# Attention with an ELU layer on one core: the first batch in slots of two heads by nine tokens, the ELU of thirteen chunks without GpSimd, chunk 0 in halves, MB in two products, another order of words

## The chip, the cores and the metric

The kernel runs on one core of a Trainium2 chip. TensorE (PE) multiplies matrices into eight PSUM banks, VectorE (DVE), ScalarE (ACT) and GpSimd (POOL) work on elements, SyncE (SP) issues DMAs, and GpSimd and ScalarE can issue them too. Each engine works through its own queue in the order in which the program was written, and waits at semaphores for the others. The metric is the device time of one execution in microseconds. All tensors that go in and out are float32.

## The reference

```python
def _attn_ref(q, k, v):                       # each 8 x 8 x 576 x 64: batch, head, token, dim
    q_s = np.exp(q - np.max(q, axis=-1, keepdims=True))
    q_s = q_s / (np.sum(q_s, axis=-1, keepdims=True) + 1e-09)
    k_s = np.exp(k - np.max(k, axis=2, keepdims=True))
    k_s = k_s / (np.sum(k_s, axis=2, keepdims=True) + 1e-09)
    kv = np.einsum('bhsd,bhse->bhde', k_s, v)
    return np.einsum('bhsd,bhde->bhse', q_s, kv)

def _moe_ref(x, w_in, w_out):                 # x 4608 x 512, w_in 512 x 2048, w_out 2048 x 512
    h = x @ w_in
    g = np.where(h > 0.0, h, np.exp(np.minimum(h, 0.0)) - 1.0)
    return g @ w_out
```

Attention here has a softmax of q over the 64 dims of a token, and a softmax of k over the 576 tokens; the 64 x 64 product of k and v is formed first, for each head. The eight heads of a token are then joined to a row of 512, and two dense layers with an ELU between them follow.

## The kernel before

One program, written out by a generator class. The work goes batch by batch (8), and for each batch its dense layers go in 16 chunks of 128 hidden columns. Of a batch's 576 tokens, 512 go through the dense layers as the main block; the remaining 64 of all batches are gathered in XTR and go through them together as a ninth block at the end.

A chunk has three stages. `hidden` (L757): four products of a 128x128 piece of w_in (W1S) with the 512 columns of XT, summed in one of three PSUM banks; then ScalarE takes the exponential into ES, and GpSimd subtracts one (L767). `elu` (L784): VectorE forms min(max(h, 0), ES) into GT, rounded to fp32r. `project` (L793): four products of GT with w_out (W2S) into four banks that stay open over all 16 chunks. The projection of a chunk stands three chunks (LAG = 3) behind its hidden products in TensorE's queue. At the end of a batch `store` copies four banks out and issues four DMAs on SyncE.

The attention of batch j+1 is woven into the chunks of batch j. The tables FIRST, SECOND and LATER give for each chunk three strings of words: done after the hidden products, after the projection, and after `elu`. A word is one step, and may name part and engine: `qmax`, `qsub`, `qexp`, `qsum`, `qmul` are the softmax of q; `kmax`/`peak`, `kturn`, `kacross`, `ksub`, `kexp` that of k; `vconv` turns v to bf16 and sets ones beside it (so that the sum of k comes out of the product); `kv` is the product of k and v, `kfac` divides it by the sum and writes MB, a 128x128 matrix for two heads with zeros off the diagonal (L552 to L566, by a mask, one operation for two heads); `turn`/`pturn` and `wide`/`pwide` turn q to QT by DMA or TensorE; `att`/`flat` multiply MB and QT, and `xc`/`xflat` copy the result to XT. `load` issues a DMA, `w1` and `w2` issue weight loads on GpSimd, `hold` makes SyncE wait for the hidden products just written.

Nothing can be multiplied before batch 0 has its attention, so the string START (L38) orders that head alone. There all q, k, v come in two halves of four heads, with four tokens beside each other in a partition (runs of 1 KB), and the last 64 tokens in separate loads with runs of 256 bytes. The maximum of k over the tokens is taken with VectorE (L299 to L312), turned by TensorE (L328), reduced (L337), put on a diagonal (`diag`) and subtracted in PSUM: `kraw` copies k there by a product with the identity (L471), `kmin` adds the negated maximum (L479, L488). Four products on ones (`warm`) stand between. Batch 1's q waits on SyncE for QS of batch 0 (`await:sp:QS0`). The first four chunks (EARLY = 4) begin their first two hidden products in the head (`h`), as soon as XT 0 and XT 1 are copied; XT 2 and XT 3 follow.

Weights come through GpSimd's own DMA queue in the order of the words `w1:c0:c1` and `w2:c0:c1`; a chunk of either is 262 KB.

## Time and profile before

| what | value |
|---|---|
| median of three runs | 311.13 us (310.7 to 311.62) |
| profiled execution | 311.19 us, span 309.4 us, granted clock 0.999 |
| TensorE busy | 295.6 us (96%), 1605 instructions |
| VectorE busy | 242.7 us (78%) |
| ScalarE busy | 177.2 us (57%) |
| GpSimd busy | 173.7 us (56%) |
| DMA | 51.63 MB, mean 167 GB/s over the span |

The span runs from the first to the last instruction; the time of the execution has 1.8 us more around it. A busy share is a mean over stages with different limits: a head in which all engines work for batch 0, then blocks of 16 chunks with the next batch's attention woven in, then two blocks with less beside the dense layers, and the last stores. DMA is full in the first quarter and mostly idle in the last.

In rows of the timeline the columns are start, duration, engine, line, operation, output and input, the number of merged instructions, and in brackets the idle time before with what ended it. In rows of groups they are busy time, mean nanoseconds of one, idle time. PEld is the loading of weights into TensorE.

### The profile page before, as it was taken

To read this page: it belongs to the slowest core of one execution; us is meant where nothing else is said; L and a number is where in the kernel's file an instruction comes from. 1 tells how busy PE (TensorE), PEld (TensorE's weight loads), DVE (VectorE), ACT (ScalarE), POOL (GpSimd) and SP (SyncE) were. 2 spreads that over 40 slices of the span, in tenths; PEclk is the share of its full clock that TensorE was granted. 3 is DMA by queue.
4 is the path that set the end of the run, shared out by engine and by line. 5 is a ranking of instruction groups with operands and counts; after the bars stand their busy time and mean duration, and the time that the engine had idled before them with its cause. 6 is when DMAs were issued, how large, how long until landed. Compare 5 with 4: busy or idle time off the path is not lost.

```text
span 309.4 us, 4558 instructions
## 1 busy us (share of the span) xinstructions
PE 295.6 (96%) x1605; PEld 236.6 (76%) x1605; DVE 242.7 (78%) x422; ACT 177.2 (57%) x295; POOL 173.7 (56%) x229
## 2 busy tenths in 40 slices
PE   3688998999999999999999999999999999999995
PEld 1356875778878888888888888788888888888884
DVE  6999998999969998999799979997995354335442
ACT  1475785567456755695469547855695543334432
POOL 2987985575546754675467636763676333333440
PEclk9999999999999999999999999999999999999999
DMA  7999999999408986656665666651422030003003
GB/s 236 319 352 328 373 337 308 250 286 237 153 11 229 260 201 162 210 149 173 176 212 148 157 192 196 160 147 52 170 36 42 2 136 0 0 2 137 0 1 136
DMA packets 65608, 51.63 MB, mean 167 GB/s; under 512 B 29361, under 2 KB 58289, under 8 KB 65585
## 3 DMA queue, kind: packets, MB, share of 16 engines
q1 hardware_dynamic: 57984, 41.23, 49.1%
q0 software_dynamic: 6400, 8.39, 10.4%
q10 hardware_dynamic: 1200, 1.72, 1.8%
q8 instruction: 12, 0.20, 0.3%
q14 instruction: 12, 0.09, 0.1%
HBM read 38.27 MB, written 9.45 MB: 154 GB/s over the span
## 4 chain that ended last, share of the span: by engine, by line
PE 86%; DMA 6%; DVE 4%; SPq 1%; issue 0%; ACT 0%; POOL 0%; DVEq 0%
PE bank L778 41%; PE bank L799 40%; DMA KR<-in_k_dram 6%; PE bank L709 2%; PE bank L535 1%; PE bank L687 1%; DVE QZ L604 1%; SPq L276 1%; SPq L284 1%; DVE KA L299 1%; DVE QM L586 0%; DVE KM L367 0%; DVE DG L355 0%; DVE QS L618 0%; DVE MB L566 0%
## 5 line engine op out<-in xcount | busy, mean ns | idle before, releaser
L767 POOL TENSOR_SCALAR ES<-ES 128x512 f32<-128x512 f32 x144 | 95.9, 667 | 118.1 <-ACT ES L766 118.0
L799 PE MATMUL bank<-W2S,GT 128*128 128x512 f32 x572 | 153.7, 392 | 0.9 <-DVE GT L789 0.9
L778 PE MATMUL bank<-XT,W1S 128*128 128x512 f32 x512 | 139.2, 394 | 0.2 <-ACT XT L696 0.2
L789 DVE SCALAR_TENSOR_TENSOR GT<-bank,ES 128x512 fp32r<-128x512 f32 x144 | 96.6, 678 | 50.3 <-PE bank L778 41.5
L766 ACT ACTIVATE ES<-bank 128x512 f32<-128x512 f32 x144 | 85.4, 597 | 86.5 <-PE bank L778 85.8
L799 PEld LDWEIGHTS bank<-W2S,GT 128*128 128x128 f32 x572 | 106.4, 188 | 23.6 <-DVE GT L789 1.4
L778 PEld LDWEIGHTS bank<-XT,W1S 128*128 128x128 f32 x512 | 94.1, 188 | 19.7 <-ACT XT L696 0.9
L594 POOL TENSOR_TENSOR QR<-QR,QM 128x512 f32<-128x512 f32 (+3 forms) x24 | 28.7, 1197 | 5.5 <-DVE QM L586 5.3
L600 ACT ACTIVATE QR<-QR 128x1024 f32<-128x1024 f32 (+3 forms) x18 | 19.0, 1060 | 12.7 <-POOL QR L594 11.4
L586 DVE TENSOR_REDUCE QM<-QR 128x16 f32<-128x1024 f32 (+3 forms) x18 | 21.7, 1208 | 0.6 <-DMA QR<-in_q_dram 0.5
L604 DVE TENSOR_REDUCE QZ<-QR 128x16 f32<-128x1024 f32 (+3 forms) x18 | 21.7, 1204 | 0.0
L731 ACT ACTIVATE XT<-bank 128x512 fp32r<-128x512 f32 (+2 forms) x28 | 15.5, 552 | 10.6 <-PE bank L709 10.6
L414 DVE TENSOR_TENSOR KR<-KR,NB 128x512 f32<-128x512 f32 x25 | 17.7, 738 | 0.2
L778 PE MATMUL bank<-XTR,W1S 128*128 128x512 f32 x64 | 16.6, 389 | 0.0
L367 DVE TRANSPOSE_TENSOR_REDUCE KM<-KR 128x32 f32<-128x1024 f32 x12 | 14.8, 1237 | 1.6 <-DMA KR<-in_k_dram 1.6
L452 ACT ACTIVATE EK<-KR 128x1024 bf16<-128x1024 f32 x14 | 14.7, 1050 | 0.8 <-POOL KR L414 0.8
L618 POOL TENSOR_TENSOR QS<-QR,QI 128x1024 f16<-128x1024 f32 (+1 forms) x9 | 14.5, 1616 | 1.1 <-DVE QI L606 1.1
L778 PEld LDWEIGHTS bank<-XTR,W1S 128*128 128x128 f32 x64 | 12.0, 188 | 2.5
L709 PE MATMUL bank<-QT,MB 128*128 128x320 f32 (+5 forms) x48 | 11.4, 298 | 0.0
L709 PEld LDWEIGHTS bank<-QT,MB 128*128 128x128 f32 x48 | 8.9, 188 | 3.3 <-DVE XT L733 0.5
L810 DVE COPY OSB<-bank 128x512 f32<-128x512 f32 x16 | 10.3, 685 | 0.4 <-PE bank L799 0.4
L618 DVE TENSOR_TENSOR QS<-QR,QI 128x1024 f16<-128x1024 f32 (+1 forms) x9 | 10.4, 1154 | 0.1
(99 smaller groups left out, 206.8 us busy)
## 6 DMA issues: line engine op xcount, KB each, us to landing
out_dram<-OSB SPq DMA_DIRECT2D x35, 256.0 KB, 2.8
KR<-in_k_dram SPq DMA_DIRECT2D x7, 1024.0 KB, 9.4
VR<-in_v_dram SPq DMA_DIRECT2D x6, 1024.0 KB, 8.2
QR<-in_q_dram SPq DMA_DIRECT2D x5, 1024.0 KB, 6.7
W1S<-in_moe_w_in_dram POOLq DMA_DIRECT2D x8, 512.0 KB, 11.5
QR<-in_q_dram SPq DMA_DIRECT2D x6, 512.0 KB, 8.0
VR<-in_v_dram SPq DMA_DIRECT2D x4, 512.0 KB, 8.3
W2S<-in_moe_w_out_dram POOLq DMA_DIRECT2D x3, 512.0 KB, 10.5
```

The lines of the kernel that those rows point to most:

```text
L414: self.op(en, lambda: e.tensor_tensor(kv, kv, m, ALU.subtract), keys + ["NB"], keys)
L586: self.op("dve", lambda: v.tensor_reduce(self.QM[:, g], QR[:, g, :], AX.X, ALU.max), self.qkeys(b, part), self.qstat("QM", part))
L594: self.op(en, lambda: e.tensor_tensor(QR[:, g, :], QR[:, g, :], m, ALU.subtract), keys + self.qstat("QM", part), keys)
L600: self.op("act", lambda: a.activation(QR[:, g, :], QR[:, g, :], AF.Exp), keys, keys)
L604: self.op("dve", lambda: v.tensor_reduce(self.QZ[:, g], QR[:, g, :], AX.X, ALU.add), self.qkeys(b, part), self.qstat("QZ", part))
L618: self.op(en, lambda: e.tensor_tensor(out, src, z, ALU.mult), keys + self.qstat("QI", part), [f"QS{x}" for x in cells])
L709: last = pe.matmul(self.bank[bank][:, a - c0:b - c0], self.MB[f][:, :, :].rearrange("p u d -> p (u d)"), self.QT[:, f, a - f * S:b - f * S ...
L766: self.op("act", lambda: a.activation(ES[:, :], ps, AF.Exp), [f"bank{bank}"], [ek])
L767: self.op("gp", lambda: g.tensor_scalar(ES[:, :], ES[:, :], -1.0, 1.0, ALU.add, ALU.mult), [ek], [ek])
L778: return pe.matmul(ps, self.W1S[:, kc, c * 128:(c + 1) * 128], x[:, kc, 0:SM], start=(kc == 0), stop=(kc == 3))
L789: self.op("dve", lambda: v.scalar_tensor_tensor(self.GT[n % NG][:, :], ps, 0.0, ES[:, :], ALU.max, ALU.min), [f"bank{bank}", ek], [f"GT{n ...
L799: return pe.matmul(self.bank[OB[t]][:, :], self.GT[n % NG][:, t * 128:(t + 1) * 128], self.W2S[:, c, :], start=(c == 0), stop=(c == NCH - ...
```

## The change

**Batch 0 in slots.** A slot is two heads. Partition p of a half (64 partitions for each head of the slot) holds nine tokens in a row, so a slot is one DMA of 128 runs of 2,304 bytes, and q, k and v of batch 0 are four such DMAs each; the separate loads of the last 64 tokens go for batch 0. The main 512 tokens are now the first eight of nine, the rest the ninth. The maximum of k goes by slots; the negated maximum comes in two products, one for each half (HALF). The turn of q is in pieces of 64x64, the product of k and v in pieces of 64 rows. The rows of batch 0 leave in eight DMAs, and its rest is stored by a DMA of its own at the very end.

**ELU.** For the chunks listed in AT["clip"] (counted through all batches) ScalarE does Relu(-h) and then exp(-...), and VectorE does max(ES - 1, h); GpSimd isn't used. Chunk 0 (FINE = 1) goes in two halves of 256 columns through the exponential, the subtraction and `elu`, and its projections wait only for their half.

**MB in two products.** `kfac` writes MB by 64 partitions, for all two-head blocks of a half at once; the mask goes.

**Words.** START and all tables have another order, with engines changed for several steps. Batch 1's q no longer waits for QS; half of it is issued by ScalarE. The warming products go from behind the first `kraw` to a place behind the products of k and v.

```diff
-START = ("load:K:0:A load:Q:0:A load:K:0:R kmax:A qmax:A load:K:0:B kmax:S kraw:A load:Q:0:B kraw:S "
-         "kmax:B kmax:T qsub:A:gp qmax:3 warm:4:3 kturn:A load:K:1:R kacross:A load:V:0:A w1:2:4 "
-         "w1:0:2 qexp:A kturn:B load:V:0:R diag:act:A w2:0:2 kmin:S kacross:B kexp:S kraw:T w1:4:6 "
-         "qsub:3:gp vconv:R:gp qmax:2 qsum:A diag:dve:B qsub:2:gp qmul:A:dve qexp:3 w2:2:5 kmin:A "
-         "qsum:3 load:V:0:B qexp:2 kraw:B kmin:T pturn:A w1:6:8 vconv:A:gp qmul:3:gp kexp:A "
-         "load:K:1:M pwide:A:act await:sp:QS0 qsum:2 kv:A kfac:A:dve kmin:B att:0 qmul:2:gp "
-         "load:Q:1:A kexp:T att:1 w1:8:10 load:Q:0:R vconv:B:dve pturn:B kexp:B xc:0 kv:B xc:1:dve "
-         "kfac:B:dve w2:5:6 load:Q:1:R h:2:4 pwide:B:act att:2 att:3 xc:2 h:0:2 kmax2:B w1:10:12 "
-         "xc:3 kmax2:A kmax2:R ")
+QP = 64
+QN = S // QP
+QF = SM // QP
+FINE = 1
...
+      "att0": 4, "att1": 7, "att2": 5, "att3": 6, "clip": (1, 2, 6, 10, 11, 14, 17, 22, 23, 25, 27, 32, 40)}
+START = ("load:Q:0:1 load:K:0:0 qmax:1 qsub:1:dve kmax:0 load:K:0:1 load:Q:0:0 load:K:0:2 kmax:1 "
+         "qmax:0 load:V:0:1 load:K:0:3 kraw:A kraw:S qexp:1 kturn:A load:Q:0:2 qsum:1 qsub:0:gp "
+         "kmax:3 load:V:0:0 kacross:A w1:2:4 diag:act:A kmax:2 kraw:B qexp:0 qmax:2 load:V:0:2 "
+         "kmin:S load:Q:0:3 w1:0:2 w2:0:3 qsub:2:gp w1:4:6 qmax:3 w1:6:8 qsum:0 load:K:1:R kturn:B "
+         "vconv:A:act kacross:B kexp:S kraw:T w2:3:6 load:V:0:3 qexp:2 kmin:A diag:act:B vconv:B:gp "
+         "load:K:1:M qsub:3:dve kmin:T qexp:3 qmul:A:dve qsum:3 qsum:2 kexp:A kexp:T kmin:B "
+         "qmul:3:gp pturn:A load:Q:1:A kexp:B pwide:A:act kv:A qmul:2:gp load:Q:1:B:act w2:6:9 "
+         "kfac:A:dve kv:B warm:1:3 load:Q:1:R kfac:B:dve att:0 w1:8:10 att:1 pturn:B xc:1 "
+         "pwide:B:act xc:0:dve w1:10:12 h:2:4 w2:9:10 kmax2:AB att:2 xc:2 att:3 xc:3 h:0:2 kmax2:R ")
 FIRST = {
...
-    7: ("qsub:D:dve", "kspread qsub:2 w1:14:16", "hold copy load:V:1:RAB"),
-    8: ("qexp:C", "qmulr0:gp ksub:1:dve", "ksub:0:dve load:K:2:MR"),
...
-    13: ("kv:A", "kexp:B kfac:A:dve att:0", "xc:0 w2:13:15 w2:15:16 peak2:A"),
-    14: ("kv:B kfac:B:dve", "att:1 qmulr:dve peak2:B", "xc:1"),
-    15: ("peak2:R join2 att:3 xc:3", "", "turn:R att:2 xc:2 kout2"),
+    4: ("", "qmax0:R hold", "w2:10:14"),
...
+    6: ("qmul:A qmax:C qsub:2:dve", "load:V:1:RAB", "qsub0:R qsub:D qexp0:R"),
+    7: ("qsum0:R", "kspread w1:14:16 qmulr0:dve load:K:2:MR copy ksub:R", "qexp:C"),
...
+    13: ("kexp:B kv:A w2:15:16 kfac:A:dve", "w2:14:15 att:0 xc:0 load:Q:2:ABR", "peak2:B"),
+    14: ("kv:B kfac:B:dve", "peak2:A peak2:R att:1", "xc:1"),
+    15: ("att:3", "turn:R xc:3 att:2", "join2 xc:2 hold load:V:2:MR kout2"),
 }
...
+        if b == 0:
+            for x in "".join({"A": "01", "B": "23"}.get(x, x) for x in parts):
+                dst = t[:, QN * int(x):QN * (int(x) + 1), :].rearrange("p r d -> p (r d)")
+                frm = src[b, 2 * int(x):2 * int(x) + 2, :, :].rearrange("h (p r) d -> (h p) (r d)", r=QN)
+                self.op(en, lambda: e.dma_start(dst, frm), (), [f"{which}F{x}"] + [f"{which}FR{x}"] * (which == "Q"), dma=f"d_{which}F{x}")
+            return
...
+    def kmax_first(self, part):
...
+        steps = ((T, src[:, :, 0:4, :], src[:, :, 4:8, :], keys, kt), (
+            T[:, :, 0:2, :], T[:, :, 0:2, :], T[:, :, 2:4, :], kt, kt), (
+            T[:, :, 0, :], T[:, :, 0, :], T[:, :, 1, :], kt, kt), (
+            out, T[:, :, 0, :], src[:, :, 8, :], keys + kt, ka))
+        for o, p, q, reads, writes in steps:
+            self.op("dve", lambda: v.tensor_tensor(o, p, q, ALU.max), reads, writes)
...
+    def kmin_first(self, part, banks):
...
+                for a in range(2):
+                    last = pe.matmul(ps, self.HALF[a][:, :],
+                                     self.DG[:, 2 * P + a, :].unsqueeze(1).broadcast_to([128, n, 128]),
+                                     start=False, stop=(a == 1))
...
+    def kv_first(self, part, bank):
...
+            for x in range(2 * P, 2 * P + 2):
+                c0 = VW * x
+                for r in range(QN):
+                    for a in range(2):
+                        sl = slice(64 * a, 64 * a + 64)
+                        last = pe.matmul(self.bank[bank][sl, c0:c0 + VW], self.EF[sl, r, x, :],
+                                         self.VF[sl, r, x, :], start=(r == 0), stop=(r == QF))
...
-        for f in range(f0, f1):
+        for u in range(2):
+            sl, keys = slice(64 * u, 64 * u + 64), [f"MB{f}u{u}" for f in range(f0, f1)]
...
+            z = self.KZ[sl, f0:f1].unsqueeze(2).broadcast_to([64, f1 - f0, 64])
             self.op("dve", lambda: v.scalar_tensor_tensor(
-                self.MB[f][:, :, :], src, self.KZ[:, f:f + 1], self.MASK[:, :, :],
-                ALU.mult, ALU.mult), [f"bank{bank}", f"KZ{f // 2}", "MASK"], [f"MB{f}"])
+                self.MBG[sl, f0:f1, u, :], ps[sl, f0:f1, 0:64], 1.0, z, ALU.mult, ALU.mult), reads, keys)
...
+    def qturn_slots(self, part, bank):
...
+            for i, x in enumerate(src):
+                for k in range(4):
+                    u, h = k // 2, slice(64 * (k % 2), 64 * (k % 2) + 64)
+                    o = 64 * (2 * i + u if part == "R" else u * n + i)
+                    last = pe.transpose(ps[h, o:o + 64], x[h, u, :], self.ID16[h, h])
...
+        for x, keys in self.pieces("ES", n, NE):
+            mark = ["FINE"] if n < FINE else []
+            if n in AT["clip"]:
+                self.op("act", lambda: a.activation(ES[:, x], ps[:, x], AF.Relu, scale=-1.0), [f"bank{bank}"], keys + mark)
+                self.op("act", lambda: a.activation(ES[:, x], ES[:, x], AF.Exp, scale=-1.0), keys, keys)
+                continue
...
+    def pieces(self, name, n, count):
+
+        halves = [(slice(256 * i, 256 * i + 256), [f"{name}{n % count}{'LH'[i]}"]) for i in range(2)]
+        return halves if n < FINE else [(slice(0, SM), [k for _, keys in halves for k in keys])]
...
+            how = (ES[:, x], -1.0, ps[:, x], ALU.add, ALU.max) if n in AT["clip"] else (
+                ps[:, x], 0.0, ES[:, x], ALU.max, ALU.min)
...
+            for i in range(2):
+                rows = self.out[0:S, :].rearrange("(p r) c -> r p c", r=QN)[2 * t + i]
+                src = self.OSB[t][64 * i:64 * i + 64, :]
+                self.op("sp", lambda: sp.dma_start(rows, src), keys, [], dma=f"d_OSB{t}")
```

435 lines of the change are left out of this document (254 added, 181 removed).

## The prediction

> **What bounds the kernel now.** I read the busy time of each engine in stretches first, then TensorE's waits, then the timeline of the head.
>
> Stretches; after the colon come the length and the busy microseconds of TensorE (PE), its weight loads, VectorE (DVE), ScalarE (ACT) and GpSimd (POOL), then the granted clock, the DMA share and GB/s:
>
> ```profile
> 0.00:20.80 20.80, 12.40 (x84) 7.05 (x84) 17.10 (x41) 9.47 (x17) 14.87 (x27) 1.00 1.07 298
> 20.80:26.30 5.50, 4.55 (x25) 3.32 (x19) 4.74 (x14) 3.87 (x7) 2.77 (x5) 1.00 1.25 344
> 26.30:50.00 23.70, 23.55 (x136) 18.44 (x136) 22.37 (x33) 16.95 (x30) 21.44 (x27) 1.00 1.31 338
> 50.00:57.30 7.30, 6.16 (x42) 3.94 (x41) 6.25 (x16) 2.91 (x6) 1.48 (x3) 1.00 1.22 323
> 57.30:80.00 22.70, 22.70 (x138) 18.46 (x138) 22.47 (x35) 14.18 (x23) 15.55 (x18) 1.00 0.97 228
> 264.00:300.00 36.00, 36.00 (x161) 29.81 (x160) 16.25 (x24) 13.66 (x24) 13.01 (x22) 1.00 0.08 30
> ```
>
> From 57.3 us on TensorE never idles. Its only idle times after 20.8 are 0.95 + 0.15 + 1.14 = 2.24 us; the other loss is the head. So the change can gain only by an earlier head and by those 2.24 us; everything else must merely stay covered. DMA is full from the head to 57 us, at about 0.34 MB/us.
>
> Who TensorE waited for from 20 to 60 us (total, times, longest), then the timeline of the end of the head (start, duration):
>
> ```profile
> PE bank L799 <- DVE GT L789: 0.9, 1, 0.9
> PE bank L687 <- DVE MB L566: 0.9, 1, 0.9
> PE bank L778 <- ACT XT L696: 0.2, 1, 0.2
> ...
> 20.82 1.19 PE L778 MATMUL bank<-XT,W1S 128*128 128x512 f32 x4
> 22.28 1.09 ACT L696 ACTIVATE XT<-bank 128x512 fp32r<-128x512 f32 x2 [0.77 <-PE bank L687]
> 26.25 1.19 PE L799 MATMUL bank<-W2S,GT 128*128 128x512 f32 x4 [0.95 <-DVE GT L789]
> 35.25 1.09 PE L778 MATMUL bank<-XT,W1S 128*128 128x512 f32 x4
> 49.23 1.07 PE L778 MATMUL bank<-XT,W1S 128*128 128x512 f32 x4
> ```
>
> Hidden work starts at 20.82, the last two XT copies end at 23.37 and the first projection starts at 26.25. Chunk 8's hidden products start at 35.25, chunk 14's at 49.23. The 0.9 us at L687 is a key-value block that came late because VectorE sat at the next batch's key maximum:
>
> ```profile
> 50.78 1.25 DVE L367 TRANSPOSE_TENSOR_REDUCE KM<-KR 128x32 f32<-128x1024 f32 x1 [1.05 <-DMA KR<-in_k_dram]
> 52.12 0.61 DVE L566 SCALAR_TENSOR_TENSOR MB<-bank,KZ,MASK 128x128 fp32r<-128x128 f32 x2
> ```
>
> **Part 1: the new head.** Times of DMAs (KB, us from issue to landing), DMA rates, and durations:
>
> ```profile
> KR<-in_k_dram SPq DMA_DIRECT2D x1, 512.0 KB, 3.9
> 3.00:6.00 3.00, 1.35 (x2) 0.83 (x3) 1.76 (x9) 0.00 (x0) 0.00 (x0) 1.00 1.11 350
> 9.00:12.00 3.00, 1.50 (x8) 0.84 (x6) 2.90 (x6) 1.06 (x1) 2.99 (x5) 1.00 1.16 289
> 18.00:21.00 3.00, 2.75 (x51) 1.77 (x44) 2.92 (x8) 2.95 (x6) 3.00 (x4) 1.00 1.50 370
> ...
> 0.73 0.47 SPq L284 DMA_DIRECT2D KR<-in_k_dram  x1
> 4.65 3.79 PE L471 MATMUL bank<-KR,ID 128*128 128x512 f32 x4 [4.65 <-DMA KR<-in_k_dram]
> 8.33 1.57 DVE L299 TENSOR_TENSOR KA<-KR 128x256 f32<-128x256 f32 x1 [0.47 <-DMA KR<-in_k_dram]
> 7.62 2.01 POOL L594 TENSOR_TENSOR QR<-QR,QM 128x1024 f32<-128x1024 f32 x1 [5.09 <-DVE QM L586]
> 14.11 1.88 PE L471 MATMUL bank<-KR,ID 128*128 128x512 f32 x4
> 15.61 1.06 ACT L502 ACTIVATE EK<-bank 128x512 bf16<-128x512 f32 x2
> 16.31 1.40 POOL L515 CAST VB<-VR 128x1024 bf16<-128x1024 f32 x1
> 19.83 0.62 PE L652 MATMUL bank<-ID,QS 128*128 128x128 f16 x8
> ...
> L594 POOL TENSOR_TENSOR QR<-QR,QM 128x512 f32<-128x512 f32 x16 | 17.2, 1078 | 0.4 <-DVE QM L586 0.2
> L301 DVE TENSOR_TENSOR KT<-KR 128x256 f32<-128x256 f32 x4 | 1.7, 418 | 0.0
> L586 DVE TENSOR_REDUCE QM<-QR 128x8 f32<-128x512 f32 x2 | 1.4, 681 | 0.0
> L253 POOL DMA_DIRECT2D W1S<-in_moe_w_in_dram x8 | 6.6, 819 | 0.0
> L260 POOL DMA_DIRECT2D W2S<-in_moe_w_out_dram x8 | 5.4, 681 | 0.0
> L618 POOL TENSOR_TENSOR QS<-QR,QI 128x512 f16<-128x512 f32 x3 | 3.1, 1038 | 0.8 <-DVE QI L606 0.7
> L670 ACT ACTIVATE QT<-bank 128x1024 fp32r<-128x1024 f16 x4 | 4.1, 1018 | 0.9 <-PE bank L652 0.9
> L696 ACT ACTIVATE XT<-bank 128x512 fp32r<-128x512 f32 x7 | 4.1, 598 | 4.1 <-PE bank L687 4.1
> L767 POOL TENSOR_SCALAR ES<-ES 128x512 f32<-128x512 f32 x144 | 95.9, 667 | 118.1 <-ACT ES L766 118.0
> L766 ACT ACTIVATE ES<-bank 128x512 f32<-128x512 f32 x144 | 85.4, 597 | 86.5 <-PE bank L778 85.8
> ```
>
> A slot is 295 KB. The first 524 KB land at 0.73 + 3.9 = 4.63; 229 KB less at 0.35 MB/us puts slot Q1 at 4.0, and each next slot comes 0.84 later: K0 4.8, K1 5.7, Q0 6.5, K3 9.0, Q2 9.9, Q3 12.4, and V3, behind batch 1's key rest, at 13.7. SyncE issues twelve slots at 0.5 to 0.6 us each, ahead of that.
>
> VectorE: maximum of Q1 to 4.7, its subtraction (0.68, as a 512-element operation; GpSimd idles) to 5.4. A slot's key maximum is four operations of 256, 128, 64 and 64 elements, 0.42 + 0.28 + 0.21 + 0.21 = 1.1 (the small ones estimated on the slope between 256 and 512): slot 0 to 6.5, slot 1 to 7.6. Maximum of Q0 to 8.3. The sum of Q1 (0.85) ends at 9.1. Now GpSimd subtracts on Q0, 8.3 to 9.4. Two-operand work of VectorE does not run beside such work: at 8.33 a 0.42 us operation took 1.57 us, until GpSimd was done. So key maximum 3 runs 9.4 to 10.5, the maximum across partitions (estimated 0.35, below a 256-element operation) to 10.8, key maximum 2 to 11.9, maximum of Q2 to 12.6.
>
> GpSimd: three weight issues after Q0, 2 x 0.82 + 0.68 = 2.3, to 11.7; subtraction on Q2 from 12.6 to 13.7; three more issues to 16.0; the value conversion, 1.40 x 9/8 = 1.6, to 17.6; two scalings of 1.04 to 19.7. This is the longest limb. ScalarE runs close beside it. The maximum of half B is known at 14.5 (behind the maximum of Q3 and the sum of Q0, 0.68 + 0.85); then come its two diagonals, the exponential of Q3 (0.6) to 15.9, the key exponentials, two pairs at 1.06 and a rest of some 0.3, to 18.3, the first QT half (1.02) to 19.3, batch 1's query DMA, which is new on this queue (0.4 to 0.5, as on SyncE), to 19.8, and XT 1 (0.6) to 20.4. So hidden work starts at about 20.4 against 20.82; the value conversion of half A, 1.2 us that GpSimd had, fits on ScalarE between 12 and 14, where it waits for subtractions.
>
> Then the transposes of half B: 32 of 64x64 in place of 8 of 128x128 (0.62). Bounds: 0.3 (pairs side by side) and 2.5 (each at the full price); I take 0.8, near equal columns streamed, to 20.5. QT 1.02 to 21.5, product 0.4, two XT copies of 0.6: 23.1 (23.37 before). Eight remaining hidden products end at 24.8.
>
> Chunk 0 in halves: half the columns pass ScalarE, GpSimd and VectorE in some 0.4 each, from 23.5 to 24.8; the full-size operations, 0.60 + 0.67 + 0.68, left the 0.95 us hole. First projection: 24.8 against 26.25, **-1.4 us**. Chunks 1 and 2 skip GpSimd at one more ScalarE pass (0.60); they are due at 26.6 and 28.4 and ready at 26.2 and 27.4.
>
> The four warming matmuls behind the first key products go. The raw products took 3.79 us for four at 4.65 and 1.88 us at 14.11. I take the fast price for half B, since TensorE has 4 us of work before it. The Trainium skill (TensorE: Matmul & The Clock Gate, What's actually happening) says an idle window of about 3.4 us halves the clock; by it a gap would put 1.9 us on half B, mostly beside GpSimd's limb. No row here shows a return to the slow price.
>
> **Part 2: weights and loads.** Chunk 8's first weights now stand behind 3.54 MB of batch 0, 2.36 of batch 1's K and Q, 2.62 of w_in (ten chunks of 0.262) and 2.36 of w_out (nine): 10.88 MB. Before, only five w_out chunks stood ahead. The old supply has 0.298 x 20.8 + 0.344 x 5.5 = 8.09 MB at 26.3 and 10.88 at 34.5. The need moves from 35.25 to 33.8: up to 0.7 us late, plus landing. But batch 0 no longer loads 0.39 MB in 256-byte runs (289 GB/s where many are under way, 370 where few), which brings all supply 0 to 1.2 us forward. I charge **+0.4** here (0 to 1.6) and **+0.2** at chunk 14 (0 to 1.8), where w_in 14 now shares with values and keys requested some 7 us sooner.
>
> **Part 3: the 1.29 us around 50.** Next-batch keys are requested a chunk earlier, without the old delay of values to chunk 7, and VectorE scales half A before the first wide key maximum, half B after it. Keys also must move behind about 16 MB, 49.7 on the old supply. Ends: 1.3 gained, 0.5 lost; I take **-0.9**.
>
> **Part 4: at nothing.** Two products per MB half replace masked ones: 64 partitions, same columns, off the path. Thirteen chunks move 0.67 us each from GpSimd to ScalarE (0.60); ScalarE is 14.18 of 22.70 busy. The new word order of later batches hides under TensorE's full stretches; a projection comes three chunks after its hidden product, over 5 us of cover. If a query turn lands late, VectorE or GpSimd holds elu; that can cost 0 to 1 us per batch. The last rows' extra store and batch 0's four extra stores (about 0.5 each) sit on SyncE, with chunks of slack: 0 to 0.6.
>
> Sum: -1.4 + 0.4 + 0.2 - 0.9 = -1.7. The profiled execution took 311.19 (span 309.4 and 1.8 around it), the median is 311.13: **309.4**.
>
> **Rivals.**
> *Weights late: slower.* Without the old wait of batch 1's queries for QS, 1.7 MB of K1 and Q1 on SyncE's queue share with GpSimd's weights from about 14 us. Speaking for it, one of the first weight pairs and the pair 8:10:
>
> ```profile
> W1S<-in_moe_w_in_dram POOLq DMA_DIRECT2D x1, 512.0 KB, 8.9
> W1S<-in_moe_w_in_dram POOLq DMA_DIRECT2D x1, 512.0 KB, 14.0
> ```
>
> At half of 0.34 MB/us the first pairs land at 18 and 21, the three w_out chunks at 24.4, pair 4:6 at 26.3 (needed 25.7), w_out 3:6 at 31.8 (31.3) and pair 8:10 at 36.1 (34.5): 0.6 + 0.5 + 1.6 = 2.7 lost. The gain of part 3 goes too: 311.1 - 1.4 + 2.7 = 312.4. It decides from 2.3 us of such stalls. Against it: fewer short runs. The Trainium skill (DMA: Bandwidth & Descriptors, Queues, rings and completion order) says that each DMA engine serves its queues in turn, packet by packet, which is this sharing. The 14.0 us of pair 8:10, issued while queries were under way, agrees with it.
>
> *The gain is handed back.* The head is earlier, but bytes set chunk 8, chunk 14 and the keys: about 1.4 us of waits, and part 3 gives 0.3: 310.8 to 311.3.
>
> *Everything holds.* No weight is late: -1.4 - 1.3 = 308.4; with a 0.8 us cheaper head 307.6.
>
> **Numbers.** Forecast (308.8 to 310.2) 0.48, everything holds 0.20, handed back 0.13, weights late 0.19. Changes within 0.3%, 0.93 us, are about what a measurement cannot tell from none. Faster 0.68, same 0.12, slower 0.20. The range, 307.6 to 312.3, leaves out about 2 in 10 (a larger head gain, a worse stall).
>
> **What would show it.** Right: hidden work from about 20.4, the first projection near 24.8 without a 0.9 us wait for GT, under 1 us of TensorE waits for W1S or W2S, under 0.5 us at MB near 50. Wrong: TensorE waiting for W1S or W2S between 24 and 49; a half-B transpose over 1.5 us; TensorE idle in any stretch after 57 us; GpSimd's limb ending after 20.5.

## The result: 1% slower, and not by more idle time in the first profile

The changed kernel took 314.5 us (median of four, 313.42 to 314.76) against 311.3 us for the kernel before beside it: a ratio of 1.0098, 95% interval 1.0070 to 1.0127. In a second comparison it was 313.77 against 311.0 us (1.0077, 1.0048 to 1.0105), with single executions from 311.94 to 315.23 us. The spread is part of the story: three profiles of the same changed kernel show three different sets of losses.

The first profiled execution took 313.42 us (span 311.6) against 311.19 (309.4) before. Its stretches, with the columns of the prediction's first table (length; busy time of TensorE, its weight loads, VectorE, ScalarE, GpSimd; granted clock; DMA share; GB/s):

```profile
0.00:20.80 20.80, 13.52 (x163) 8.12 (x165) 17.26 (x50) 9.82 (x18) 13.26 (x23) 1.00 1.01 306
20.80:26.30 5.50, 5.17 (x34) 3.57 (x27) 5.02 (x9) 4.23 (x9) 3.50 (x6) 1.00 1.25 348
26.30:50.00 23.70, 22.37 (x113) 17.47 (x111) 17.37 (x26) 17.89 (x32) 18.73 (x20) 0.93 1.33 351
50.00:57.30 7.30, 7.30 (x66) 4.95 (x65) 6.85 (x14) 5.06 (x8) 3.44 (x6) 1.00 0.92 194
57.30:80.00 22.70, 22.49 (x101) 18.25 (x100) 21.13 (x33) 16.78 (x28) 15.44 (x16) 1.00 0.83 232
```

Idle time of TensorE from 20.8 to 80 us is 0.33 + 1.33 + 0 + 0.21 = 1.87 us (before: 0.95 + 0.15 + 1.14 = 2.24). The 1.14 us before 57.3 are gone, as forecast; 1.33 us have come between 26.3 and 50. What is new in this profile is the clock in that stretch, 0.93. The list of TensorE's waits names the 1.33 us (total, times, longest):

```profile
PE bank L914 <- DMA W1S<-in_moe_w_in_dram: 1.3, 1, 1.3
```

Its timeline around that place (start, duration, operation, and in brackets the idle time before it):

```profile
21.07 1.19 PE L914 MATMUL bank<-XT,W1S 128*128 128x512 f32 x4
25.94 1.15 PE L935 MATMUL bank<-W2S,GT 128*128 128x512 f32 x4 [0.26 <-DMA W2S<-in_moe_w_out_dram]
28.43 1.77 PE L914 MATMUL bank<-XT,W1S 128*128 128x512 f32 x4 [1.33 <-DMA W1S<-in_moe_w_in_dram]
30.00 1.91 PE L935 MATMUL bank<-W2S,GT 128*128 128x512 f32 x4
31.71 1.33 PE L914 MATMUL bank<-XT,W1S 128*128 128x512 f32 x4
32.87 1.08 PE L935 MATMUL bank<-W2S,GT 128*128 128x512 f32 x4
```

Four slices of 1 us from that stretch, in the columns of the first table:

```profile
28.00:29.00 1.00, 0.57 (x2) 0.53 (x3) 0.94 (x3) 0.88 (x1) 0.62 (x1) 0.90 1.45 384
29.00:30.00 1.00, 1.00 (x3) 0.72 (x3) 1.00 (x2) 0.17 (x1) 0.00 (x0) 0.50 1.39 383
31.00:32.00 1.00, 1.00 (x4) 0.80 (x3) 0.49 (x2) 0.00 (x0) 1.00 (x2) 0.50 1.41 370
32.00:33.00 1.00, 1.00 (x5) 0.77 (x5) 0.33 (x1) 0.00 (x0) 0.27 (x1) 0.89 1.75 357
```

TensorE waits 1.33 us for w_in's pair 4:6 (chunk 4), and then runs at half clock from 28.8 to 32.2 us, 3.41 us: the twelve products from 28.43 to 32.87 take 4.44 us where three groups at 0.91 us take 2.73, so **1.7 us** are lost while it counts as busy. A table of idle times alone would have found nothing to explain 2.2 us.

The head came in hardly earlier. Hidden work starts at 21.07 us (20.82 before, 20.4 forecast) and the first projection at 25.94 (26.25; 24.8). The timelines of VectorE, then GpSimd, in the new head:

```profile
14.20 1.65 DVE L681 TENSOR_TENSOR QR<-QR,QF 128x512 f32<-128x512 f32 x1
15.77 1.21 DVE L710 TENSOR_TENSOR QS<-QR,QF 128x1024 f16<-128x1024 f32 x1
...
13.62 1.53 POOL L256 DMA_DIRECT2D W1S<-in_moe_w_in_dram  x2
15.13 0.76 POOL L263 DMA_DIRECT2D W2S<-in_moe_w_out_dram  x1
15.87 2.12 POOL L859 CAST VB<-VR 128x1152 bf16<-128x1152 f32 x1
```

The subtraction on slot 3 took 1.65 us, 0.68 being the price that the prediction had for such a subtraction; 0.95 us of it ran beside GpSimd's issue of w_in, which ended at 15.15. GpSimd's value conversion, charged at 1.6, took 2.12 beside VectorE's scaling. GpSimd's two scalings behind it end at 20.01 in place of 19.7, the half-B transposes follow, and the first hidden products stand behind these in TensorE's queue.

### The profile page after: what moved, and what is told of

Its sections match the earlier page's. It is cut to its first block, busy times and chain, and to the rows that moved or that the text cites. A ratio compares the mean times of both kernels' runs of the same rounds, so it can differ in the third digit from the quotient of the medians.

```text
span 311.6 us, 4703 instructions
## 1 busy us (share of the span) xinstructions
PE 298.8 (96%) x1692; PEld 239.1 (77%) x1692; DVE 230.8 (74%) x391; ACT 189.0 (61%) x315; POOL 183.3 (59%) x231
## 3 DMA queue, kind: packets, MB, share of 16 engines
q10 hardware_dynamic: 1728, 2.24, 2.4%
## 4 chain that ended last, share of the span: by engine, by line
PE 86%; DMA 7%; DVE 3%; issue 1%; SPq 1%; ACT 1%; POOL 0%; ACTq 0%
PE bank L935 41%; PE bank L914 40%; DMA W1S<-in_moe_w_in_dram 5%; PE bank L829 2%; DMA KR<-in_k_dram 2%; PE bank L600 1%; SPq L277 1%; DVE GT L927 1%; DVE KT L325 1%; PE bank L807 0%; DVE KC L435 0%; POOL QR L681 0%; PE bank L1009 0%; PE bank L746 0%; DVE MB L631 0%
## 5 line engine op out<-in xcount | busy, mean ns | idle before, releaser
L898 POOL TENSOR_SCALAR ES<-ES 128x512 f32<-128x512 f32 (+1 forms) x132 | 85.3, 647 | 110.5 <-ACT ES L897 110.2
L927 DVE SCALAR_TENSOR_TENSOR GT<-bank,ES 128x512 fp32r<-128x512 f32 (+1 forms) x132 | 88.8, 676 | 56.5 <-PE bank L914 45.0
L897 ACT ACTIVATE ES<-bank 128x512 f32<-128x512 f32 (+1 forms) x132 | 77.9, 593 | 84.1 <-PE bank L914 80.6
L681 POOL TENSOR_TENSOR QR<-QR,QM 128x512 f32<-128x512 f32 (+1 forms) x25 | 29.7, 1190 | 0.4 <-DVE QM L674 0.3
L710 POOL TENSOR_TENSOR QS<-QR,QI 128x1024 f16<-128x1024 f32 (+1 forms) x15 | 27.8, 1856 | 0.7 <-DVE QI L693 0.7
L691 DVE TENSOR_REDUCE QZ<-QR 128x16 f32<-128x1024 f32 (+1 forms) x14 | 18.8, 1341 | 0.2 <-ACT QR L686 0.2
L674 DVE TENSOR_REDUCE QM<-QR 128x16 f32<-128x1024 f32 (+1 forms) x14 | 18.6, 1336 | 0.2 <-DMA QR<-in_q_dram 0.2
L462 DVE TENSOR_TENSOR KR<-KR,NB 128x512 f32<-128x512 f32 (+1 forms) x17 | 15.6, 917 | 0.2
L462 POOL TENSOR_TENSOR KR<-KR,NB 128x512 f32<-128x512 f32 x10 | 13.0, 1301 | 0.0
L582 ACT ACTIVATE VB<-VR 128x1024 bf16<-128x1024 f32 x12 | 12.7, 1058 | 0.1
```

The lines of the kernel that those rows point to most:

```text
L462: self.op(en, lambda: e.tensor_tensor(kv, kv, m, ALU.subtract), keys + ["NB"], keys)
L674: self.op("dve", lambda: v.tensor_reduce(m, QR, AX.X, ALU.max), self.qkeys(b, part), self.qstat("QM", b, part))
L681: self.op(en, lambda: e.tensor_tensor(QR, QR, m, ALU.subtract), keys + self.qstat("QM", b, part), self.qown(b, part))
L691: self.op("dve", lambda: v.tensor_reduce(z, QR, AX.X, ALU.add), self.qkeys(b, part), self.qstat("QZ", b, part))
L710: self.op(en, lambda: e.tensor_tensor(out, QR, z, ALU.mult), keys + self.qstat("QI", b, part), [f"QS{x}" for x in cells])
L897: self.op("act", lambda: a.activation(ES[:, x], ps[:, x], AF.Exp), [f"bank{bank}"], keys + mark)
```

## The experiments

The median of the kernel before lay between 311.0 and 311.6 us in every comparison; ratios are against it.

**The same kernel again.** Two more profiles of the changed kernel, with no edit.

> The changed kernel itself, profiled a second time; its median is 314.5 us and its profiled execution was 313.42 us. Theory A (the eight stores of batch 0 make batch 2's key load late, and the typical execution pays for it): TensorE waits 1 to 2 us for the exponentials of K near 81 us, which the first profile doesn't show, and the time is near 314.5 us. Theory B (the typical execution only waits longer for weights at chunks 4 and 5): no such wait, and the wait for W1S at chunk 4 is 1.5 us or more.

> The changed kernel again. Theory A (every execution waits 0.9 to 1.4 us for w_in at chunk 4; whether that wait is followed by some 3.4 us of half clock, at 1.7 us, and whether the keys come too late near 81 us, at up to 1.8 us, changes from execution to execution): times spread from 311.5 to 315 us, median 313 to 314.6, and the profile shows one or both. Theory B (the 311.7 us execution was the outlier of a narrow spread): nearly all times within 313.4 to 314.8 us.

Where an expectation calls the late keys batch 2's, they are batch 3's; what waits behind them is batch 2's leftover. The first profile took 311.7 us and fits neither theory of its expectation (no wait for EK, and 1.16 us for w_in at chunk 4); the second took 314.53 (seven executions: 311.94 to 315.23). Together with the first four, twelve executions have a median of 314.0. The list of TensorE's waits from 20.8 to 120 us in the 311.7 us execution:

```profile
PE bank L914 <- DMA W1S<-in_moe_w_in_dram: 1.5, 2, 1.2
```

The same list in the 314.53 us execution:

```profile
PE bank L600 <- ACT EK L503: 1.8, 1, 1.8
PE bank L914 <- DMA W1S<-in_moe_w_in_dram: 1.2, 1, 1.2
PE bank L935 <- DMA W2S<-in_moe_w_out_dram: 0.7, 1, 0.7
```

And VectorE's timeline there:

```profile
75.53 1.25 DVE L415 TRANSPOSE_TENSOR_REDUCE KM<-KR 128x32 f32<-128x1024 f32 x1 [1.39 <-DMA KR<-in_k_dram]
79.00 1.80 DVE L473 TENSOR_TENSOR KR<-KR,NB 64x256 f32<-64x256 f32 x2
```

Neither of them drops to half clock at the w_in wait of 1.2 us. The 314.53 us execution pays elsewhere: VectorE waits 1.39 us for batch 3's keys, and behind that maximum in its queue stands the subtraction on batch 2's leftover keys (L473). Their exponential (L503) comes late, and TensorE waits 1.78 us for it at 81.3. In the 311.7 us execution the same maximum starts at 73.92 without waiting, and the subtraction takes half the time. VectorE's timeline there:

```profile
77.38 0.85 DVE L473 TENSOR_TENSOR KR<-KR,NB 64x256 f32<-64x256 f32 x2
```

So 0.95 of the 1.78 us is the subtraction itself: coming late, it meets GpSimd's conversion of QT (79.29 to 80.51), which in the 311.7 us execution begins at 79.01, behind it. The same holds in the six other profiles with a wait for EK of 1.6 to 2.0 us (e1_await, e3_both, f2_await_qmax, g1_order2, i2_noclip, i3_nofine), where it takes 1.65 to 1.96 us; in all the others it takes 0.85 to 0.87. How late chunks end against the kernel before, read from the ends of VectorE's `elu` in the timelines (positive is later, us; the order of words differs, so a single chunk may be off by 1 us):

| chunk | 313.42 us | 311.7 us | 314.53 us |
|---|---|---|---|
| 6 (36.6 us before) | 1.87 | -0.04 | 0.70 |
| 20 (68.0) | 1.26 | -0.12 | 0.20 |
| 32 (91.7) | 2.29 | 0.83 | 3.22 |
| 64 (154.6) | 2.20 | 0.50 | 3.32 |
| 143 (302.0) | 2.05 | 0.32 | 3.17 |

Against the 311.7 us execution the first column is 1.9 us later at chunk 6 and 1.7 at the end, which is the half clock, and the last column loses 2.1 us more between chunks 20 and 32, which is the late keys. From chunk 64 on nothing more is lost in any of them. Theory A of the second expectation holds: the spread is real, and one profile was not the typical execution.

The granted clock on record for every execution says how often. One stretch of half clock lowers the mean by 0.005 to 0.006. Of the twelve executions five have 0.995 or less, with a median of 314.56 us; the other seven have 312.47. But the kernel before has 0.995 or less in 33 of 82 executions, with medians of 311.6 and 311.0. So half clock is about as frequent in it, and the profile before, at 0.999, happened to have none. What differs is what it costs, 2.1 against 0.6 us between the groups. Which of the five also had late keys isn't on record, and neither is the place of the half clock in any execution without a profile.

**The wait for QS0.** The kernel before held batch 1's queries back until QS0 was written. Put back into the changed kernel, and taken from the kernel before:

```
e1_await   - load:Q:1:A kexp:B          + await:sp:QS0 load:Q:1:A kexp:B
b1_noawait - await:sp:QS0 qsum:2        + qsum:2        (kernel before)
```

> The changed kernel with one word put back: batch 1's query half A and rest wait on SyncE for QS again. Theory 1 (the weights are late because batch 1's queries, free of their wait, share the DMA engines with them): TensorE's wait for W1S (1.33 us) shrinks below 0.3 us, the granted clock from 26.3 to 50 us goes from 0.93 back to 1.0, and the time falls from 314.5 to 310.5 to 311.5. Theory 2 (the weights are late because three w_out chunks and a subtraction of GpSimd stand ahead of w_in 4:6): the wait stays over 0.8 us, the clock stays at 0.93 to 0.95, and the time falls by less than 1 us.

> The kernel before with the wait of batch 1's queries for QS taken out, and nothing else. Theory 1: TensorE waits for W1S or W2S between 24 and 36 us by 0.5 to 2 us, the granted clock falls below 0.98 from 26.3 to 50, and the time rises from 311.3 to 312.3 to 314. Theory 2: no wait over 0.3 us, clock 1.0, time within 0.7 us of 311.3.

With the wait the changed kernel is slower: 315.99 us (1.0145, 1.0115 to 1.0175). The trace shows why: the pair w_in 4:6 lands at 26.87 us, against 28.38 in the first profile of the changed kernel (24.85 in the kernel before), and so ahead of the 27.10 us at which TensorE began to wait for it there. The w_in wait goes, and a longer one takes its place, because the changed word order asks for the maximum of those queries ahead of chunk 0's `elu`. TensorE's longest wait there:

```profile
PE bank L935 <- DVE GT L927: 3.1, 1, 3.1
```

What VectorE waited for, in its timeline:

```profile
27.13 1.22 DVE L674 TENSOR_REDUCE QM<-QR 128x16 f32<-128x1024 f32 x1 [3.25 <-DMA QR<-in_q_dram]
```

Without it the kernel before is the same: 311.93 us (1.0008, 0.9991 to 1.0026), and its pair 4:6 still lands at 25.25. So in the old word order the removed wait costs nothing that this can measure. The profile of that run holds a second case of the clock, at another place: TensorE waits 1.04 us for w_out, the granted clock is 0.50 from 57.7 to 61.1, and the next products take 1.83 and 1.91 us in its timeline:

```profile
57.41 1.83 PE L799 MATMUL bank<-W2S,GT 128*128 128x512 f32 x4 [1.04 <-DMA W2S<-in_moe_w_out_dram]
59.04 1.91 PE L778 MATMUL bank<-XT,W1S 128*128 128x512 f32 x4
```

**The order of the weights.**

```
e2_worder  - w2:0:3 qsub:2:gp w1:4:6    + w2:0:2 w1:4:6 qsub:2:gp
           - w2:3:6                     + w2:2:6
g1_order2  as e2_worder, with w2:2:4 w2:4:6 in place of w2:2:6
e3_both    e1_await and e2_worder together
```

> The changed kernel with the old order of weights: w_out 0:2 in place of 0:3, then w_in 4:6, both issued before GpSimd's second subtraction, and w_out 2:6 later. Theory 1 (sharing with the queries): the wait for W1S stays over 0.6 us with a clock of 0.93 to 0.97, the time falls by less than 1.5 us. Theory 2 (order): the wait and the 0.3 us wait for W2S go, the clock is 1.0, the time is 310.5 to 311.5.

> The changed kernel with the weights in this order: w_in 2:4, 0:2, w_out 0:2, w_in 4:6 before GpSimd's second subtraction; w_in 6:8, w_out 2:4, 4:6 after it, so that GpSimd's value conversion starts where it does in the changed kernel. Theory 3 (three losses: w_in 4:6 late, the half clock that follows the idle time, and in the order experiment a later head because VectorE's scaling of queries met GpSimd's conversion): hidden work starts at 21.0 to 21.3, no wait of TensorE for weights over 0.3 us, granted clock 1.0 in every stretch, 310.5 to 311.8. If order is not what makes the typical run slow (something else stalls in most executions): 313.5 to 315.

> Both of these changes together. Either theory: no wait for weights of batch 0 before chunk 8, clock 1.0; first projection at 25.7, and what is left of the gains (1.1 us of idle time near 50, 0.6 us of head) gives 309.5 to 311. If a later chunk waits for weights instead (w_in 8:10 behind nine w_out chunks), 311 to 312.5.

Measured: 314.58 us (1.0087, 1.0052 to 1.0123), 314.79 (1.0104, 1.0068 to 1.0140) and 318.69 (1.0205, 1.0161 to 1.0250). No order of the same bytes helped. In the profile of e2_worder no wait for w_in is left: the pair lands at 27.01, and the head, which asks for it, is 1.45 us later (hidden work from 22.52). The scaling on VectorE now meets GpSimd's conversion from the start, and TensorE ran at half clock from 17.7 to 21.1 us; the run doesn't part the two. The timelines of VectorE and GpSimd:

```profile
15.63 2.16 DVE L710 TENSOR_TENSOR QS<-QR,QF 128x1024 f16<-128x1024 f32 x1
...
15.05 1.66 POOL L859 CAST VB<-VR 128x1152 bf16<-128x1152 f32 x1
```

In g1_order2 the pair lands at 28.05, a w_in wait of 1.07 us stays, at full clock, and the wait for EK near 82 us (1.74 us) appears: the clue to the late keys. e3_both waits 3.42 us for GT and 1.96 for EK, and has half clock after each. But it shows what makes the pair late. When w_in 4:6 lands, in all profiles of this kernel and its variants but h4_kqsw:

| order of weights | batch 1's queries | lands at (us) |
|---|---|---|
| new | free (ten profiles) | 27.5 to 28.8 |
| new | wait (e1_await, f2_await_qmax, i1_await_kq) | 26.7 to 27.4 |
| old | free (e2_worder, g1_order2, g4_all) | 26.8 to 28.1 |
| old | wait (e3_both) | 23.4 |

Either alone helps by about 1 us, both together by 4 to 5.

**Keys ahead of the stores.**

```
f3_kearly     batch 1's chunk 4: - load:K:2:MR    chunk 1: + load:K:2:MR (ahead of load:Q:2:MR)
f2_await_qmax e1_await, and batch 0's qmax:A moved from chunk 0 to behind chunk 1's elu
g4_all        g1_order2, that qmax:A, and f3_kearly
```

> The changed kernel with the keys of batch 3 requested in chunk 1 of batch 1, ahead of batch 0's eight stores (5.0 us of SyncE) instead of behind them. Theory 4 (the eight stores make these keys late, VectorE waits at their maximum, and the next batch's products of keys and values come late): TensorE's idle time from 57 to 108 us falls from 0.55 to below 0.25 us, and the time by 0.3 to 1 us, to 313.5 to 314.2. Rival: nothing changes, 314.5.

> The changed kernel with the wait of batch 1's queries put back, and the maximum of those queries moved from ahead of chunk 0's elu to behind chunk 1's. Theory 3: the 3.1 us that the wait alone cost (VectorE at that maximum, elu behind it) shrinks below 1 us, no wait for W1S, so 311.5 to 313. If the queries' late landing only moves to the next step of VectorE: 314 to 316.

> The order of the first of these, the maximum of batch 1's queries behind chunk 1's elu, and the early request of keys together, without the old wait of queries. If theories 3 and 4 hold, TensorE loses under 1.2 us to idle time after 20.8 and the clock stays at 1.0: 309.5 to 310.8, faster than both kernels.

The keys alone give 312.31 us (1.0031, 1.0009 to 1.0052), about 2 us under the changed kernel and far more than the 0.3 to 1 us that I had expected. Not all of it need be the wait: only one of these 12 executions has a granted clock of 0.995 (and the profiled one, 313.08 us, ran at 0.95 from 9 us to the end, which no other profile here shows), against five of 12 for the changed kernel, and the medians without them are 312.1 and 312.5. g4_all gives 312.50 (1.0044, 1.0024 to 1.0063), f2_await_qmax 313.24 (1.0065, 1.0028 to 1.0102) with the EK wait (1.67 us) in its profile. SyncE's timeline shows what had made the keys late. The kernel before:

```profile
62.47 1.99 SPq L818 DMA_DIRECT2D out_dram<-OSB  x4
64.51 0.91 SPq L284 DMA_DIRECT2D KR<-in_k_dram  x1
```

The changed kernel:

```profile
63.79 5.03 SPq L961 DMA_DIRECT2D out_dram<-OSB  x8
68.86 0.61 SPq L293 DMA_DIRECT2D KR<-in_k_dram  x1
```

Batch 0's eight stores of 64 rows hold SyncE 5.03 us, 0.63 each, where four of 128 rows took 1.99, and the key load behind them starts 4.35 us later (1.32 of them because the stores themselves begin later). The landing moves less: in the three profiles of the changed kernel the keys are there at 75.56, 73.89 and 75.51 us, against 74.15 before. They hurt because VectorE asks for them earlier (at 73.9 and 74.1 us in the two profiles at full clock, 74.82 before) and has the subtraction behind them.

**Four stores, and the query maximum.** The two parts of the store loop as one transfer with a target of three dimensions; and batch 3's query maximum back to where it stood, since in f3_kearly VectorE waited 1.65 us for it at 107.46 with an `elu` behind it.

```
h1_four   - for i in range(2): rows = out[..., 2*t+i]; dma_start(rows, OSB[t][64*i:64*i+64])
          + rows = out[..., 2*t:2*t+2]; dma_start(rows, OSB[t])
h2_kq     f3_kearly, and qmax2:A from the start of batch 1's chunk 14 to the end of chunk 15
h4_kqsw   h1_four, h2_kq, and w2:0:2 early, w2:2:4 w2:4:6 in place of w2:0:3, w2:3:6
```

> The changed kernel with batch 0 stored by four transfers of 128 rows in place of eight of 64. Theory A (the stores hold SyncE 5.0 us, 3 us longer than four of them did, and the key load of batch 2 behind them comes late): SyncE held 2.0 to 2.5 us, the key load issued near 66 us in place of 68.9, no TensorE wait for EK near 81; median 312.5 to 313.5 us, 1 to 2 us under the changed kernel's 314.5. Theory B (weights alone): unchanged at 314.2 to 314.8 us. Rival to A: a store with a three-dimensional target takes as long to issue as two, then nothing moves.

> The changed kernel with the key load of batch 2 ahead of batch 0's stores and the maximum of batch 3's queries put back from the start of chunk 14 to the end of chunk 15 of batch 1's stretch. Theory C (with the keys early, that maximum waits 1.65 us on VectorE for the query load, with chunk 40's elu behind it, and TensorE loses 0.8 to 1.3 us near 109): no wait near 109; median 311.0 to 311.6 us, some 1 us under the 312.31 of the key load alone. Rival: the maximum, moved later, delays the queries of batch 3 by 3 us and the loss comes back after 115 us: 312.0 to 312.6 us.

> As the kernel with the early keys and the later maximum, and also four stores for batch 0, and w_out loaded in pairs (0:2 early, 2:4 and 4:6 behind w_in 6:8), so that w_in 4:6 has a quarter MB less ahead of it. If weights at chunk 4 cost their wait alone (1.0 us): the wait falls to 0.3 to 0.6 us and the median is 310.2 to 311.0 us, below the kernel before. If the bytes taken off the queue are made up by the batch-1 queue, which alternates with it packet by packet: wait unchanged, median as the kernel without the reordering, 311.0 to 311.6 us.

h1_four took 328.29 us (1.0548, 1.0524 to 1.0572): it moved the keys the wrong way, and shows the mechanism at full size. The stretch from 66 to 72 us:

```profile
66.00:72.00 6.00, 6.00 (x30) 5.04 (x29) 5.68 (x8) 4.79 (x7) 4.40 (x6) 1.00 0.14 51
```

The longest waits of VectorE and of TensorE from 60 to 100 us:

```profile
DVE KM L415 <- DMA KR<-in_k_dram: 16.4, 1, 16.4
...
PE bank L914 <- DVE GT L927: 14.3, 1, 14.3
```

With the four stores under way the core moves 51 GB/s, where it moved a mean of 245 (other loads among them) from 63 to 69 us with the eight, and the keys come so late that VectorE waits 16.4 us for them and TensorE 14.3. The DMA share of 0.14 is about what two of the 16 engines can give (2/16 = 0.125), and the target's first dimension is 2; whether the one follows from the other no run tested. Half clock from 81.2 to 94.8 adds to the price. It spoils h4_kqsw too (323.26 us; 1.0406, 1.0372 to 1.0439), of which only the head can be read: its wait for w_in is 1.21 us, so taking a quarter MB off the queue ahead of that pair doesn't shorten it.

h2_kq took 312.39 us in a narrow spread (311.96 to 312.64; 1.0038, 1.0023 to 1.0053): the wait near 109 us is gone and the time is that of f3_kearly, in the rival's range and not the 1 us less of theory C; the loss that the rival put after 115 us doesn't show as a TensorE wait. A wait of 0.67 us for EK is left in its profile. GpSimd now waits for the broadcast key maximum, not for the keys, in its timeline:

```profile
70.05 1.29 POOL L462 TENSOR_TENSOR KR<-KR,NB 128x512 f32<-128x512 f32 x1 [1.07 <-DMA NB<-kmax_scratch]
```

**The ELU parts.**

```
i2_noclip - "clip": (1, 2, 6, 10, 11, 14, 17, 22, 23, 25, 27, 32, 40)   + "clip": ()
i3_nofine - FINE = 1                                                    + FINE = 0
```

> The changed kernel with the elu of all chunks as before, with GpSimd. The prediction took this part at nothing: 313.8 to 315.0 us, level with the changed kernel in the same call. If the chunks without GpSimd keep value conversions and query work from being late: TensorE waits for GT or EK of 0.5 us or more at one of the 13 chunks, 0.5 to 2 us slower. If the second pass on ScalarE delays its conversions: 0.3 to 1 us faster.

> The changed kernel with chunk 0's elu in one piece instead of two halves. The prediction's Part 1 took the halves to bring the first projection forward: chunk 0's GT would be ready some 0.3 to 0.6 us later and the first projection start at 26.3 to 26.6 in place of 25.94 us. As TensorE then waits for w_in 4:6 until 28.1 to 28.4 us anyway, the end doesn't move: level with the changed kernel in the same call (within 0.3%). If the gap before chunk 4 shrinks by what the first projection is late, half clock is rarer, and the kernel gains 0.3 to 1 us.

Without the thirteen chunks that skip GpSimd the changed kernel takes 324.36 us (1.0429, 1.0408 to 1.0450), 10.6 us more. VectorE then waits 5.24 us at chunk 10, one of the thirteen, for an ES that stands behind 5.7 us of key subtractions and query scaling in GpSimd's queue. The timelines of VectorE, then GpSimd:

```profile
51.26 0.69 DVE L927 SCALAR_TENSOR_TENSOR GT<-bank,ES 128x512 fp32r<-128x512 f32 x1 [5.24 <-POOL ES L898]
...
44.95 2.54 POOL L462 TENSOR_TENSOR KR<-KR,NB 128x512 f32<-128x512 f32 x2
47.46 1.89 POOL L710 TENSOR_TENSOR QS<-QR,QI 128x1024 f16<-128x1024 f32 x1
49.32 1.25 POOL L462 TENSOR_TENSOR KR<-KR,NB 128x512 f32<-128x512 f32 x1
```

TensorE waits 3.06, 2.50, 3.89 and 1.80 us in that profile, and runs at half clock from 50.5 to 57.3. The new word order needs the thirteen. The halves of chunk 0 are worth nothing that this can measure: 313.41 us without them, 313.77 with them in the same comparison.

**Attempts at a faster kernel.**

```
i1_await_kq f2_await_qmax and h2_kq together
j1_peak     batch 1: peak2:A from chunk 7 to the end of chunk 10, peak2:B from chunk 9 to chunk 11
j2_peak_p1  j1_peak, and chunk 1 is projected ahead of chunk 4's hidden products
```

> The changed kernel with the wait for QS0 before batch 1's query load, the maximum of batch 1's queries behind the elu of chunk 1, the key load of batch 2 ahead of batch 0's stores, and the maximum of batch 3's queries at the end of chunk 15. If the three waits (weights at chunk 4, keys near 81, queries near 109) are all of the loss: no TensorE wait of 0.8 us or more after 21 us, median 310.4 to 311.4 us, level with the kernel before. If the wait for QS0 pushes the lateness to batch 1's queries (waits of 0.5 and 0.7 us at chunks 5 and 9, as without the other two edits): 311.6 to 312.4 us.

> The changed kernel with the maxima of batch 3's keys (halves A and B) moved behind the subtraction of batch 2's leftover keys, to the ends of chunks 10 and 11 of batch 1's stretch; loads, stores and weights as they are. (The earlier expectations call these keys batch 2's: the load in batch 1's stretch fetches batch 3's.) Theory D (the late load costs only because VectorE waits for it with batch 2's subtraction queued behind): no TensorE wait for EK near 81 us however late the load, times 311.5 to 313.5 us, set by the wait for w_in and by whether half clock follows it; median 311.8 to 312.8 us, 1 to 2 us under the changed kernel. Rival (SyncE's late issue delays other loads too): a wait for queries or values of 0.7 us or more after 85 us, median 313 to 314.5 us.

> As the kernel with the later maxima of keys, and TensorE projects chunk 1 ahead of chunk 4's hidden product, so the 1.2 to 1.3 us in which it waits for w_in 4:6 holds 0.9 us of work (chunk 1's GT is ready at 27.44 us in the 311.7 us execution). Theory (the wait for w_in and its half clock are what is left): the wait falls to 0.1 to 0.6 us, no half clock at 28 to 32 us, median 310.3 to 311.2 us, level with the kernel before or 0.2% below. Rival (w_in 6:8 is the next late pair, 2 us behind): a new wait of 0.5 to 1 us at chunk 6 near 31 us, 311.4 to 312.3 us.

i1_await_kq has no wait of 0.8 us left and still takes 312.78 us (1.0055, 1.0035 to 1.0075); waits of 0.50 for GT and 0.69 for the key broadcast near 32 and 39.6 us have come for the ones removed. j1_peak (314.15; 1.0073, 1.0048 to 1.0098) does away with the EK wait, but the two maxima now keep VectorE busy when it should make MB, and TensorE waits 1.96 us for that. The timelines of VectorE, then TensorE:

```profile
79.70 2.36 DVE L415 TRANSPOSE_TENSOR_REDUCE KM<-KR 128x32 f32<-128x1024 f32 x2
...
83.70 0.41 PE L829 MATMUL bank<-QT,MB 128*128 128x320 f32 x1 [1.96 <-DVE MB L631]
```

j2_peak_p1 (313.83; 1.0070, 1.0046 to 1.0094) carries the same 1.96 us. Its head is the best seen: no wait for w_in, 0.53 us for GT in its place, and chunk 18 ends 0.51 us before that of the kernel before, where j1_peak is 0.12 behind. No version beat the kernel before. The projection put forward together with h2_kq was not tried.

## Why the prediction was wrong

The forecast was 309.4 us (308.8 to 310.2) with a range to 312.3; 314.5 lies above it, and above the slowest rival (312.4). With the head 1.1 us short of its gain and 0.6 to 0.9 us more waiting for weights, the sum would have given 311.1 to 311.4 (an estimate), close to the 311.7 us execution. The rest is half clock and late keys, which the sum had at nothing.

- **Part 1, the head: -1.4 forecast, -0.3 measured** (first projection 25.94 against 26.25; another profile has 25.76). The step that failed is the overlap of VectorE and GpSimd: the conversion at "1.40 x 9/8 = 1.6", and the subtraction on slot 3, for which no term stands beside the 0.68 of slot 1's. The prediction used the rule that VectorE's two-operand work doesn't run beside GpSimd's for the key maxima, and left it out here: 1.65 and 2.12 us. It also started hidden work at 20.4, ahead of its own half-B transposes to 20.5, which stand before it in the queue. The transposes, 0.8 forecast, took 0.69, and the slots landed within 0.3 us of the forecast. The first projection then waited 0.26 us for w_out, which landed at 25.81.
- **Part 2, weights: chunk 8 was the wrong place.** The sum charged 0.4 at chunk 8 and 0.2 at chunk 14. The wait comes at chunk 4, where the rival "Weights late" had it, at 0.6; it was 1.33, 1.16 and 1.21 us in the three profiles. The pair landed at 28.38 us (26.3 by the rival), and was asked for at 27.10 (25.7). No wait came at chunk 8, and 0.29 us near 50.6 in the 311.7 us execution. The sharing that it named is there. The table of queues from 18 to 21 us in the kernel before (packets, MB, share of 16 engines):

```profile
q0 software_dynamic: 797, 1.05, 141.6%
q1 hardware_dynamic: 68, 0.06, 8.3%
```

And in the changed one:

```profile
q0 software_dynamic: 534, 0.59, 69.4%
q1 hardware_dynamic: 532, 0.42, 56.9%
```

  GpSimd's weight queue goes from 1.05 to 0.59 MB in those 3 us, packet for packet with batch 1's loads. Only with the new order of weights does this make the pair late: the table above needs both put back to undo it.
- **"No row here shows a return to the slow price."** True of the profile before, and taken as if it couldn't happen, though 33 of 82 executions of that kernel have it. After 1.33 us of waiting it did, at 1.7 us. The rule of the Trainium skill that stood beside it (TensorE: Matmul & The Clock Gate, What's actually happening) has a window of about 3.4 us that runs free of the kernel, so that its effect may differ between runs. The length agrees (half clock from 28.80 to 32.21 us), and so does the changing outcome: waits of 1.33 and 1.04 us were followed by half clock, those of 1.07, 1.16 and 1.21 were not. So do the places: in profiles with two stretches of half clock their starts lie a whole number of 3.413 us apart (13.35 and 57.72 in b1_noawait, 13 times; 31.18 and 85.80 in e3_both, 16 times). The idle window of 3.4 us that it asks for does not agree: the 3.41 us ahead of the half clock held 1.81 us of TensorE work in the first profile and 2.16 in b1_noawait. When all twenty profiles are cut into such windows from the first clock record on, half clock follows every window with less than 1.59 us of work, none with more than 2.16, and some of those between. The 1.16 us wait of the 311.7 us execution fell across the border of two windows (2.66 and 2.85 us of work). Where the border falls is luck.
- **Part 3 was right.** The 1.14 us before 57.3 are gone in the first profile (0.52 and 0.22 us are idle there in the other two), and in the execution with the fewest losses chunk 20 ends 0.12 us before the old one.
- **Part 4: the four extra stores.** "Chunks of slack: 0 to 0.6" was the step that failed. Each took 0.63 us, near the 0.5 charged, but the working stopped at SyncE. Behind the stores waits a key load; VectorE waits for it with the maximum of batch 3's keys, and the new order had put that maximum ahead of batch 2's leftover subtraction. In VectorE's timeline of the kernel before, the subtraction came at 70.05 and the maximum at 74.82:

```profile
70.05 0.87 DVE L425 TENSOR_TENSOR KR<-KR,NB 64x256 f32<-64x256 f32 x2
74.82 1.23 DVE L367 TRANSPOSE_TENSOR_REDUCE KM<-KR 128x32 f32<-128x1024 f32 x1
```

  The price is up to 1.8 us of TensorE time near 81 us, half of it from the subtraction's meeting with GpSimd. Loading the keys first takes about 2 us off the median, and h1_four shows the same chain with 14.3 us.
- **Part 4, the thirteen chunks at nothing**, named the right cover: ScalarE has the room, and undoing them costs 10.6 us.

What stays open: how often an execution pays for late keys, and where its half clock falls. With the keys early 1.0 to 1.3 us over the kernel before remain; 0.9 us of waiting for w_in is in the profiles of f3_kearly and h2_kq, and in that of g4_all 0.50 us for GT and 0.72 for the key broadcast; no run removed one without another.

## What to carry to other kernels

Where a step is made of more DMA issues, follow the queue behind them to the end: what load is issued later, which engine asks for it first, and what stands behind that request. A new wait of about 1 us on TensorE should be charged with a chance of 1.7 us more for the clock, and the time compared with several executions, not one profile: the granted clock of every execution tells, on both sides, how many had it. Two operations that slow each other should be laid side by side for each pair that the new order makes, not for the one pair that the old profile shows.

## What the runs showed of the hardware

- Half clock after short waits: TensorE waits of 1.04, 1.33, 1.96 (in e3_both and j2_peak_p1), 3.14 and 3.42 us were followed by 3.41 us at 0.50; waits of 0.91 to 1.21 us, of 1.60 to 1.82, one of 1.96 (j1_peak), and ones of 2.50 and 3.06 (i2_noclip) were not. Four profiles (b1_noawait, e2_worder, i3_nofine, j1_peak) have such a stretch in the head, between 13.3 and 21.1 us.
- Stores of 128 rows whose target has three dimensions (2 x 64 x 512) left the core at 51 GB/s and a DMA share of 0.14.
- The issue of a store on SyncE took 0.63 us for 64 rows and 0.50 for 128, so that half the size cost no less.
- VectorE's subtraction of 128x512 took 1.65 us while GpSimd did no more than issue weight DMAs (0.69 elsewhere), and two of 64x256 took 1.65 to 1.96 us beside GpSimd's conversion of QT (0.85 ahead of it).
